# The last two output writes of a retention and soft-MoE kernel, each cut into two transfers by rows

## The chip, the cores and the metric

The kernel runs on one core of one Trainium2 chip. The metric is the device time of one execution in microseconds; lower is better.

## The reference

Two layers follow each other. The first is a linear attention with a decay per head (4 batches, 8 heads, 768 positions, 64 wide); the second is a soft mixture of experts over all 3072 tokens, with 8 experts of 4 slots each.

```python
state = gamma * state + k_t v_t^T          # per batch, head and position t
y_t   = scale * q_t @ state
x      = y as (3072 tokens, 512)
logits = x @ phi                           # 32 slots
d = softmax of logits over the tokens;  slot_input = d.T @ x
h = max(slot_input[e] @ w1[e], 0);      slot_out[e] = h @ w2[e]     # 8 experts
c = softmax of logits over the slots;   out = c @ slot_out          # (3072, 512)
```

## The kernel before, in words

The order of every engine's work is the order of the code (a manual schedule over all engines). All data moves by transfers that SyncE (SP) issues from one queue; the ones that concern us are writes of 128 partitions from SBUF to the output in HBM.

The first part of the kernel steps through the 24 pieces of the attention (4 batches by 6 chunks of 128 positions) in pairs and gathers the slots' inputs on the way; the weights `w1` and `w2` stream in beside this. Then come the experts: `hidden` (line 586) is the first layer, and the second layer is cut into three blocks of output columns, `BLOCKS` (line 36), of 256, 128 and 128. A block's second layer is 64 matmul groups into one bank (line 669). When a block is summed, the generator `finish` (line 630) takes it: it copies the sum, spreads it with one matmul (line 638), and then combines it with the weights `cT`: for each 128 output columns (`m`) and each half of the tokens (`h`) four matmuls of 384 columns (line 650), four copies out of PSUM by VectorE and ScalarE in turn (line 655) into one SBUF tile `ot` of 128 x 1536, and one write of that tile (line 656). The output in HBM is laid out with the 512 columns as rows and the 3072 tokens along a row, so each write moves 128 rows of 6144 bytes. There are 8 such writes: 4 of the first block, 2 of the second, 2 of the third. The writes of a block are spread among the matmuls of the next block; those of the third block have nothing after them.

The program ends (line 733, the end of the kernel's context) when SP has seen every transfer land and the engines have met.

Of the kernel before, what the change touches and what calls it, by code (L numbers as in the profile page):

```python
# [17 lines left out]
C = 128  # L18
# [17 lines left out]
BLOCKS = [(0, 256), (256, 128), (384, 128)]  # L36
# [8 lines left out]
PACE = (1, 1, 1, 2, 1, 2, 1, 2, 2, 0, 2, 2)  # L45
TURNED = (0, 1, 2, 3, 4, 8, 12, 14)
SIW = 48
LEAN = [i for i in range(1, NSTEP) if i in TURNED or i >= NSTEP - B]
FULL = [i for i in range(1, NSTEP) if i not in LEAN]

# [31 lines left out]
def retention_soft_moe_kernel(  # L82
# [9 lines left out]
    nc = tc.nc  # L92
# [11 lines left out]
    def large(pool):  # L104
        return pool.tile([128, 2048], F32, name="b", tag="b")

    def slot():
        return ring.tile([128, 1024], F32, name="r", tag="r")

    def small(name, shape, bufs=1):  # L110
        return cpool.tile(shape, F32, name=name, bufs=bufs)

    def bank(name, shape=(128, 512)):
        return ps.tile(list(shape), F32, name=name)
# [73 lines left out]
    def load_in(i):  # L188
# [5 lines left out]
        if i == 0:  # L194
            nc.sync.dma_start(t[:, 0:1024], first_[0])
            nc.sync.dma_start(first, first_[1])
            st[i]["v"] = first[:, K_ALL:K_ALL + 512].rearrange("p (h e) -> p h e", e=D)
        elif i in LEAN:
            nc.sync.dma_start(t[:, 0:1536], in3[LEAN.index(i)])
        else:  # L200
# [329 lines left out]
    weight_pool[0] = big  # L530
    siT = qtab.rearrange("p g t -> p (g t)")[:, 0:2 * (NK * SIW + 16)]
    nc.gpsimd.memset(siT, 0.0)
    siT = siT.rearrange("p (g x) -> p g x", g=2)
    sis = siT[:, :, 0:NK * SIW].rearrange("p g (k s) -> p g k s", s=SIW)[:, :, :, 0:16]
    si0 = qtab.rearrange("p g t -> p (g t)")
# [50 lines left out]
    def hidden(hf, g, k):  # L586
        for j in range(4):
            a = g * NK * SIW + k * SIW + 4 * j
            nc.tensor.matmul(hp[hf][32 * j:32 * j + 32, :], si0[:, a:a + NSLOT],  # L589
# [40 lines left out]
    def finish(cb, op):  # L630
        c0, w = BLOCKS[cb]
        os_ = small("os", [128, 256])
        s4 = slot()
        nc.vector.tensor_copy(os_[:, :w], op[:, :w])
        for _ in range(Y1[cb] - 1):
            yield
        rp = bank("Y0")
        nc.tensor.matmul(rp[:, :w], rep, os_[:, :w], start=True, stop=True)  # L638
        nc.vector.tensor_copy(s4[:, :w], rp[:, :w])
        for _ in range(Y2[cb] - 1):  # L640
            yield
        for m in range(w // 128):
            for h in range(2):
                ot = large(big)[:, 0:12 * C].rearrange("p (c j t) -> p c j t", j=B, t=C)
                cps = []
                for j in range(B):
                    tags = co_tags if cb < len(BLOCKS) - 1 else last_tags
                    cp = bank(tags[n_co[0] % len(tags)]).rearrange("p (c t) -> p c t", t=C)[:, 0:3]
                    n_co[0] += 1
                    nc.tensor.matmul(cp, s4[32 * j:32 * j + 32, m * 128:(m + 1) * 128],  # L650
                                     cT[32 * j:32 * j + 32, 3 * h:3 * h + 3, :], start=True, stop=True,
                                     skip_group_check=True, tile_position=(32 * j, 0))
                    cps.append(cp)
                for j in range(B):
                    (nc.scalar.copy if j % 2 else nc.vector.tensor_copy)(ot[:, :, j, :], cps[j])
                nc.sync.dma_start(out[c0 + m * 128:c0 + (m + 1) * 128, h * 12 * C:(h + 1) * 12 * C],
                                  ot.rearrange("p c j t -> p (c j t)"))
                for _ in range(BURST[cb]):
                    yield

    for cb, (c0, w) in enumerate(BLOCKS):
        if cb == len(BLOCKS) - 1:
            n_co[0] = 0
        op = bank(("A0", "A1")[cb % 2])
        units = ([(g, 4 * hf + f) for hf in range(2) for g in range(2) for f in range(4)] if cb == 0 else
                 [(g, fc) for g in range(2) for fc in range(NFC)])
        for n, (g, fc) in enumerate(units):
            for j in range(4):
                nc.tensor.matmul(op[32 * j:32 * j + 32, :w], hT[fc // 4][:, fc % 4, 4 * g + j, :],  # L669
                                 w2t[4 * g + j, cb, fc], start=(n == 0), stop=(n == len(units) - 1),  # L670
                                 skip_group_check=True, tile_position=(0, 32 * j))
            if cb == 0 and n == 2:
                hidden_t(1)
            for f in pend:
                next(f, None)
        done = finish(cb, op)
        next(done)
        for f in pend:
            for _ in f:
                pass  # L680
        pend = [done]
# [4 lines left out]
def lay_out(q, k, v, moe_phi, moe_w1, moe_w2):  # L686
# [6 lines left out]
    def nat(x):  # L693
        x = np.asarray(x).reshape(B, H, NC, C, D)
        return x.transpose(2, 0, 3, 1, 4).reshape(NSTEP, C, 512)
# [7 lines left out]
    for cb, (c0, w) in enumerate(BLOCKS):  # L703
# [3 lines left out]
        else:  # L707
# [3 lines left out]
    x = np.concatenate([kt, qt, vn, nat(k)], axis=2)  # L711
    return dict(x3=x[LEAN][:, :, 0:1536], x4=x[FULL],
                w1=w1, w2=np.concatenate(w2),
# [24 lines left out]
```

## Time and profile before

| what | before |
|---|---|
| median of 3 runs | 158.36 us (158.28 to 158.56) |
| the profiled execution's own time | 158.41 us |
| its span, first to last instruction | 156.6 us |
| TensorE busy | 144.6 us (92%) |
| DMA engines, mean share of 16 from 5 to 148 us | 0.99 to 1.02 |
| last instruction of VectorE that computes ends | 149.13 us |
| last output write issued, landed | 149.19 us, 155.5 us |

The span is what the views of the trace show; the execution's own time is 1.8 us longer. A share of the 16 DMA engines of 1.0 means that all sixteen move data; 0.5 is eight of them, 0.19 three.

### The profile page before, as it was taken

The page shows a single profiled execution, that of the slowest core. Times are in us where ns is not written, and L with a number is a line of the kernel's source. Part 1 is how long each engine was busy: PE and PEld are TensorE (multiplying, and loading weights), DVE is VectorE, ACT ScalarE, POOL GpSimd, SP SyncE. Part 2 cuts the span into 40 slices and gives each one's busy share as a digit, 9 for nine tenths or more (in the row PEclk, how much of TensorE's full clock was granted, in tenths as well). Part 3 has the DMA queues.
Part 4 walks back from the last instruction along what each step waited for, and adds up shares of the span by engine and source line. Part 5 has one row for each costly group of instructions (what it writes and reads, how often), then busy time and mean ns, then how long its engine had stood idle before and what let it go on. Part 6 is the DMA issues. An engine that isn't in the chain of part 4 may idle for free.

```text
span 156.6 us, 5484 instructions
## 1 busy us (share of the span) xinstructions
PE 144.6 (92%) x2412; PEld 107.4 (69%) x2412; DVE 77.8 (50%) x187; ACT 42.2 (27%) x100; POOL 58.8 (38%) x66
## 2 busy tenths in 40 slices
PE   7999999999999999999999979999999999999500
PEld 2688989897988789979996857864232555557200
DVE  0379337682865483768574847566010104535500
ACT  3215422333232316220613042344100001424300
POOL 1351986784936294654938283010000000000000
PEclk9999999999999999999999999999999999999985
DMA  4999999999999999999999999999999999999891
GB/s 159 421 424 421 416 419 416 416 414 419 406 423 408 423 419 410 427 398 431 404 419 412 415 411 416 400 408 421 411 428 416 423 416 416 414 415 417 348 402 78
DMA packets 9816, 62.48 MB, mean 399 GB/s; under 512 B 1088, under 2 KB 1088, under 8 KB 4544
## 3 DMA queue, kind: packets, MB, share of 16 engines
q1 hardware_dynamic: 9792, 62.13, 96.6%
q8 instruction: 19, 0.31, 0.8%
q14 instruction: 5, 0.04, 0.1%
HBM read 55.84 MB, written 6.29 MB: 397 GB/s over the span
## 4 chain that ended last, share of the span: by engine, by line
PE 92%; DVE 2%; issue 1%; DVEq 0%
PE A L227 16%; PE Y L260 15%; PE A L669 9%; PE A L304 7%; PE Y L251 6%; PE S L288 6%; PE Y L589 4%; PE A L589 4%; PE sm L328 4%; PE sm L424 3%; PE S L384 3%; PE A L206 2%; PE sm L650 2%; PE S L650 1%; PE Y L650 1%; PE Y L638 1%
## 5 line engine op out<-in xcount | busy, mean ns | idle before, releaser
L235 DVE TENSOR_TENSOR r<-A,mi 128x512 f32<-128x512 f32 (+1 forms) x50 | 30.1, 662 | 22.1 <-PE A L227 22.1
L212 POOL TENSOR_TENSOR b<-b,qtab 128x512 f32<-128x512 f32 x20 | 25.7, 1287 | 23.5 <-DMA b<-in_x_dram 18.3
L227 PE MATMUL A<-b 64*128 64x128 f32 x384 | 25.4, 280 | 0.0
L227 PEld LDWEIGHTS A<-b 64*128 64x128 f32 x384 | 22.7, 188 | 3.1 <-issue 2.0
L217 POOL TENSOR_TENSOR b<-b,kt 128x512 f32<-128x512 f32 x23 | 23.6, 1046 | 2.4 <-DMA b<-in_x_dram 2.4
L260 PE MATMUL Y<-r,b 128*64 128x128 f32 x352 | 22.5, 276 | 0.5 <-issue 0.5
L260 PEld LDWEIGHTS Y<-r,b 128*64 128x64 f32 x352 | 19.2, 137 | 2.9 <-issue 2.6
L669 PE MATMUL A<-b,r 128*32 128x128 f32 (+1 forms) x336 | 15.9, 300 | 0.0
L311 ACT COPY r<-A 128x512 f32<-128x512 f32 x23 | 12.4, 592 | 8.6 <-PE A L304 8.6
L669 PEld LDWEIGHTS A<-b,r 128*32 128x32 f32 x336 | 10.3, 109 | 6.4 <-issue 4.4
L304 PE MATMUL A<-mi,r 128*128 128x128 f32 x96 | 13.3, 278 | 0.3 <-ACT r L279 0.3
L288 PE MATMUL S<-b 128*64 128x64 f32 x304 | 11.1, 222 | 0.6 <-issue 0.6
L304 PEld LDWEIGHTS A<-mi,r 128*128 128x128 f32 x96 | 10.4, 141 | 1.7 <-ACT r L279 0.5
L288 PEld LDWEIGHTS S<-b 128*64 128x64 f32 x304 | 10.4, 138 | 0.5 <-issue 0.5
L251 PE MATMUL Y<-b,sst 64*64 64x128 f32 x304 | 10.6, 276 | 0.0
L416 POOL TENSOR_TENSOR cn<-cn,cz 128x128 f32<-128x128 f32 x6 | 2.4, 401 | 19.6 <-DVE cz L415 7.2
L280 DVE COPY r<-Y 128x512 f32<-128x512 f32 x9 | 6.2, 690 | 5.9 <-PE Y L260 5.1
L251 PEld LDWEIGHTS Y<-b,sst 64*64 64x64 f32 x304 | 8.2, 132 | 1.2
L328 PEld LDWEIGHTS sm<-r,kt 128*32 128x32 f32 x192 | 6.2, 110 | 3.3 <-issue 3.3
L408 ACT ACTIVATE cn<-cn 128x128 f32<-128x128 f32 x6 | 1.9, 310 | 21.2 <-DVE cn L407 21.2
L328 PE MATMUL sm<-r,kt 128*32 128x128 f32 x192 | 7.4, 273 | 0.0
L297 DVE TENSOR_TENSOR sst<-sst,S 128x256 f32<-128x256 f32 x16 | 6.0, 418 | 2.7 <-PE S L288 2.5
(140 smaller groups left out, 182.9 us busy)
## 6 DMA issues: line engine op xcount, KB each, us to landing
b<-in_w_dram SPq DMA_DIRECT2D x29, 1024.0 KB, 15.1
b<-in_x_dram SPq DMA_DIRECT2D x12, 1024.0 KB, 12.5
b<-in_x_dram SPq DMA_DIRECT2D x11, 768.0 KB, 10.7
out_dram<-b SPq DMA_DIRECT2D x8, 768.0 KB, 8.7
r<-in_w_dram SPq DMA_DIRECT2D x5, 512.0 KB, 11.0
b<-in_first_dram SPq DMA_DIRECT2D x1, 512.0 KB, 3.5
r<-in_first_dram SPq DMA_DIRECT2D x1, 512.0 KB, 4.3
sst<-in_w_dram SPq DMA_DIRECT2D x1, 512.0 KB, 11.7
```

The costliest lines, as they stand in the source:

```text
L212: nc.gpsimd.tensor_tensor(q, q, qtab, ALU.mult)
L217: nc.gpsimd.tensor_tensor(v, v, vsc[:, i // B, a:b].unsqueeze(2).broadcast_to([128, b - a, D]), ALU.mult)
L227: nc.tensor.matmul(s["sc"][r][:, g, :], s["kT"][half(r), g, :], s["qT"][half(r), g, :], start=True, stop=True, skip_group_check=True)
L235: nc.vector.tensor_tensor(s["A"][:, r, g:g + n], s["sc"][r][:, g:g + n], mask.unsqueeze(1).broadcast_to([128, n, C]), ALU.mult)
L251: nc.tensor.matmul(p["y"][k][b][half(half_of(r, g)), gl, :], sst[(2 * P + k) % B][half(r), g, :], s["qT"][half(r), g, :], start=(gl == 0 a ...
L260: nc.tensor.matmul(pr[P]["y"][k][g // 2][half(half_of(r, g)), g % 2, :], s["v"][:, 2 * g + r, :], s["A"][:, r, g, :], start=(P < B // 2 an ...
L288: nc.tensor.matmul(S_[half(r), k, g, :], s["kn"][:, 2 * g + r, :], s["v"][:, 2 * g + r, :], start=True, stop=True, skip_group_check=True)
L304: nc.tensor.transpose(X[k][:, g * 128:(g + 1) * 128], pr[P]["yT"][:, k, g, :], ident)
L311: (nc.scalar.copy if engines[k] == "scalar" else nc.vector.tensor_copy)(xn, pr[P]["X"][k])
L328: nc.tensor.matmul(q["ltp"][32 * j:32 * j + 32, :], phis[:, p, :], st[GRP * g + j]["yT"][:, p, :], start=(p == 0), stop=(p == NPAIR - 1), ...
L589: nc.tensor.matmul(hp[hf][32 * j:32 * j + 32, :], si0[:, a:a + NSLOT], w1t[hf, g, k][:, j * 512:(j + 1) * 512], start=(g == 0 and k == 0), ...
L669: nc.tensor.matmul(op[32 * j:32 * j + 32, :w], hT[fc // 4][:, fc % 4, 4 * g + j, :], w2t[4 * g + j, cb, fc], start=(n == 0), stop=(n == le ...
```

## The change

The third block's two writes are cut by rows into two transfers each. For the half `h` = 0 (the write ahead of the last) the cut is at row 104: transfers of 104 and 24 rows. For `h` = 1 (the last) it is at row 120: transfers of 120 and 8 rows. What is written, and from which tile, is the same; the other six writes are as before.

```diff
+LAST_ROWS = (104, 120)
...
-                nc.sync.dma_start(out[c0 + m * 128:c0 + (m + 1) * 128, h * 12 * C:(h + 1) * 12 * C],
-                                  ot.rearrange("p c j t -> p (c j t)"))
+                cuts = (0, 128) if cb < len(BLOCKS) - 1 else (0, LAST_ROWS[h], 128)
+                for a, b in zip(cuts, cuts[1:]):
+                    nc.sync.dma_start(out[c0 + m * 128 + a:c0 + m * 128 + b, h * 12 * C:(h + 1) * 12 * C],
+                                      ot[a:b].rearrange("p c j t -> p (c j t)"))
```

On SP's queue the end of the program stood as follows before: four writes of the first block, two of the second and two of the third. The name in front of the arrow is the output, `b_...` is the tile `ot`, and the brackets name what SP waits for ahead of the issue; DMAHW0 to DMAHW7 are eight landing semaphores, taken in turn.

```order
L656 DMA out_0_dram<-b_1908 128x1536 [waits DMAHW4_49,DVE_49,Activation_49]
L656 DMA out_0_dram<-b_1934 128x1536 [waits DMAHW5_49,DVE_49,Activation_49]
L656 DMA out_0_dram<-b_1960 128x1536 [waits DMAHW6_49,DVE_49,Activation_49]
L656 DMA out_0_dram<-b_1986 128x1536 [waits DMAHW7_49,DVE_49,Activation_49]
L656 DMA out_0_dram<-b_2035 128x1536 [waits DMAHW0_49,DVE_49,Activation_49]
L656 DMA out_0_dram<-b_2061 128x1536 [waits DMAHW1_49,DVE_49,Activation_49]
L656 DMA out_0_dram<-b_2113 128x1536 [waits DMAHW2_49,DVE_49,Activation_49]
L656 DMA out_0_dram<-b_2127 128x1536 [waits DMAHW3_49,DVE_49,Activation_49]
```

The same place on SP's queue with the change; the line numbers are those of the changed file.

```order
L659 DMA out_0_dram<-b_1908 128x1536 [waits DMAHW4_49,DVE_49,Activation_49]
L659 DMA out_0_dram<-b_1934 128x1536 [waits DMAHW5_49,DVE_49,Activation_49]
L659 DMA out_0_dram<-b_1960 128x1536 [waits DMAHW6_49,DVE_49,Activation_49]
L659 DMA out_0_dram<-b_1986 128x1536 [waits DMAHW7_49,DVE_49,Activation_49]
L659 DMA out_0_dram<-b_2035 128x1536 [waits DMAHW0_49,DVE_49,Activation_49]
L659 DMA out_0_dram<-b_2061 128x1536 [waits DMAHW1_49,DVE_49,Activation_49]
L659 DMA out_0_dram<-b_2113 104x1536 [waits DMAHW2_49,DVE_49,Activation_49]
L659 DMA out_0_dram<-b_2113 24x1536 [waits DMAHW3_49]
L659 DMA out_0_dram<-b_2128 120x1536 [waits DMAHW4_49,DVE_49,Activation_49]
L659 DMA out_0_dram<-b_2128 8x1536 [waits DMAHW5_49]
```

The last two rows of before have become four. The second part of each waits for no copy of its own, only for a landing semaphore's earlier use; the 120-row part has moved from the semaphore DMAHW3 to DMAHW4. No other engine's instructions change.

## Rows read from the trace of the kernel before

**Rows 1.** The page's first and second part: busy time of the engines, and the span in 40 slices of 3.9 us, with the mean busy share of the 16 DMA engines in tenths and the rate that they moved.
```profile
PE 144.6 (92%) x2412; PEld 107.4 (69%) x2412; DVE 77.8 (50%) x187; ACT 42.2 (27%) x100; POOL 58.8 (38%) x66
...
DMA  4999999999999999999999999999999999999891
GB/s 159 421 424 421 416 419 416 416 414 419 406 423 408 423 419 410 427 398 431 404 419 412 415 411 416 400 408 421 411 428 416 423 416 416 414 415 417 348 402 78
```

**Rows 2.** The end of the program in stretches (from:to in us): length, busy time of PE, PEld, DVE, ACT, POOL, granted TensorE clock, mean share of the 16 DMA engines, GB/s.
```profile
144.00:146.00 2.00, 1.43 (x38) 0.97 (x29) 0.41 (x2) 0.00 (x0) 0.00 (x0) 1.00 1.01 421
146.00:147.00 1.00, 0.77 (x12) 0.54 (x15) 0.18 (x1) 0.00 (x0) 0.00 (x0) 1.00 0.99 412
147.00:148.00 1.00, 0.80 (x12) 0.19 (x4) 0.82 (x2) 0.78 (x3) 0.00 (x0) 1.00 0.70 281
148.00:149.00 1.00, 0.00 (x0) 0.00 (x0) 1.00 (x3) 0.84 (x3) 0.00 (x0) 1.00 0.55 221
149.00:150.00 1.00, 0.00 (x0) 0.00 (x0) 0.13 (x1) 0.00 (x0) 0.00 (x0) 1.00 0.96 399
150.00:151.00 1.00, 0.00 (x0) 0.00 (x0) 0.00 (x0) 0.00 (x0) 0.00 (x0) 1.00 1.02 418
```

**Rows 3.** The same columns in short stretches of the last microseconds.
```profile
152.20:152.80 0.60, 0.00 (x0) 0.00 (x0) 0.00 (x0) 0.00 (x0) 0.00 (x0) 0.50 0.98 399
152.80:153.03 0.23, 0.00 (x0) 0.00 (x0) 0.00 (x0) 0.00 (x0) 0.00 (x0) 0.50 0.59 241
153.10:153.33 0.23, 0.00 (x0) 0.00 (x0) 0.00 (x0) 0.00 (x0) 0.00 (x0) 0.50 0.51 214
153.33:153.56 0.23, 0.00 (x0) 0.00 (x0) 0.00 (x0) 0.00 (x0) 0.00 (x0) 0.50 0.20 80
153.60:153.83 0.23, 0.00 (x0) 0.00 (x0) 0.00 (x0) 0.00 (x0) 0.00 (x0) 0.50 0.19 80
154.40:154.63 0.23, 0.00 (x0) 0.00 (x0) 0.00 (x0) 0.00 (x0) 0.00 (x0) 0.50 0.19 80
154.70:154.93 0.23, 0.00 (x0) 0.00 (x0) 0.00 (x0) 0.00 (x0) 0.00 (x0) 0.50 0.13 53
154.93:155.20 0.27, 0.00 (x0) 0.00 (x0) 0.00 (x0) 0.00 (x0) 0.00 (x0) 0.50 0.06 23
155.20:156.60 1.40, 0.00 (x0) 0.00 (x0) 0.00 (x0) 0.00 (x0) 0.00 (x0) 0.50 0.00 0
```

**Rows 4.** The last two writes: the timeline of SP (start, length, line and operation), and the view of line 656 from 147 us on (its two issues' durations, and the times from issue to landing).
```profile
148.26 1.26 SPq L656 DMA_DIRECT2D out_dram<-b  x2
L656 SPq DMA_DIRECT2D out_dram<-b x2: 332/332/333, 148.3 to 149.2; - x2
DMA to landing us min/median/max: 5.4/5.9/6.3
```

**Rows 5.** The timeline of VectorE and ScalarE, the last copies of line 655 (start and length).
```profile
147.65 1.48 DVE L655 COPY b<-A 128x384 f32<-128x384 f32 x3
148.33 0.51 ACT L655 COPY b<-Y 128x384 f32<-128x384 f32 x1
```

**Rows 6.** The waits of SP's queue from 140 us on, and the semaphore instructions of the program's end (line 733) on SP, with the first and last start.
```profile
SPq L733 <- DMA out_dram<-b: 6.0, 1, 6.0
L733 SPq EVENT_SEMAPHORE  x7: 17/28/28, 155.5 to 156.5; - x7
```

**Rows 7.** The page's third part: packets of all transfers by size, and by queue the packets, megabytes and share of 16 engines over the span.
```profile
DMA packets 9816, 62.48 MB, mean 399 GB/s; under 512 B 1088, under 2 KB 1088, under 8 KB 4544
## 3 DMA queue, kind: packets, MB, share of 16 engines
q1 hardware_dynamic: 9792, 62.13, 96.6%
q8 instruction: 19, 0.31, 0.8%
q14 instruction: 5, 0.04, 0.1%
```

## The prediction

> **What bounds the kernel now.** I read the page's slices first, then the end of the program in ever shorter stretches. The reader should see in [rows 1] that the DMA engines are full from the second slice nearly to the end, and the last slice is almost empty; TensorE is busy for 92% of the span, but the stretch that this change touches comes after its last matmul. In [rows 2] compute stops at about 149.1 us and DMA goes on alone. The last two writes are issued at 148.26 and 149.19 us and land 5.4 and 6.3 us later, at 153.7 and 155.5 [rows 4]. SP waits 6.0 us for that landing and needs 1.1 us more to end the program [rows 6]. So whatever the last landing moves, the time moves, as long as nothing else gets later than it.
>
> The short stretches [rows 3] show how the drain ends. The share of the 16 engines is 0.98 until 152.8, then 0.51 (8 engines), from 153.33 on 0.20 and 0.19 (3 engines), and this until past 154.7. So eight engines are done at about 153.0, five at about 153.5, and three at about 155.1. More than a quarter of the time from 149.1 to 155.1 is spent with three engines of sixteen. Thirteen engines have nothing to do for the last 1.5 us or more: this is the time that can be won.
>
> Why three are late: of the 16 engines' time 0.8% goes to 19 instruction blocks [rows 7], 0.008 x 16 x 156.6 / 19 = 1.06 us each on one engine. The late three stand 2.1 us behind the first eight, which is two such blocks. While the queue is full the engines never meet, so such a delay stays; only when the early ones run dry, as in 147 to 149 us with shares of 0.70 and 0.55 [rows 2], do they wait for the next write. [...]
>
> **What a row costs.** Three engines move 80 GB/s together [rows 3], so 6144 bytes take 6144 / 26.7 GB/s = 0.23 us on one engine. All 68 transfers of before have 128 rows and end in 1088 small packets, 16 each; 9792 - 1088 = 8704 = 68 x 128 are data [rows 7]. A write is thus sixteen shares of 8 rows, 1.84 us each.
>
> **What the change does to the shares.** No row shows a transfer of other than 128 rows. I assume that it is cut into equal shares of whole rows, on as many engines up to 16 as divide it, counted from the lowest: 104 = 13 x 8, 24 = 12 x 2, 120 = 15 x 8, 8 = 8 x 1. [...] Against the 16 rows per engine of the two writes of before:
> - engines 0 to 7: 8 + 2 + 8 + 1 = 19 rows, +3, +0.69 us
> - engines 8 to 11: 18 rows, +2, +0.46 us
> - engine 12: 16 rows, no change
> - engines 13 and 14: 8 rows, -1.84 us
> - engine 15: none, -3.68 us
>
> The bounds of this term are the split that changes nothing (all sixteen share, 0 us) and the one above.
>
> **The sum.** If the three late engines are 13 to 15, they finish at 155.1 - 1.84 = 153.3 or sooner. The five end at 153.5 + 0.46 = 154.0 at most if they are 8 to 12, the eight at 153.0 + 0.69 = 153.7. The last engine is then done at 154.0 in place of 155.1: -1.1 us. If one of the five is among those with three more rows it is 154.2, -0.9 us; if the five took nothing at all, 153.5 would be the floor, -1.6 us.
>
> Two more issues of 0.33 us stand on SP [rows 4]. The 24 rows are issued right behind the 104, from 148.6 to 148.95 us, before the last tile's copies end at 149.13 [rows 5], so the 120 rows go out at 149.19 as before. If that cover were gone it would cost up to 0.33 us of issue, but not of landing, since all engines are full at 150 to 151 [rows 2]. The 8 rows go out near 149.55, more than 3 us before an engine reaches them. The new waits are for landing semaphores of earlier writes; DMAHW4 and DMAHW5 were last used by the first two output writes, which a queue this full has finished well before 148 us. Those cost 0. Behind the last of them stands only the end of the program.
>
> Against the profiled execution's 158.41 us the sum is 158.41 - 1.1 = 157.3; its median of three is 0.05 lower, which leaves 157.3 us after rounding. About 0.2% (0.3 us) is what a measurement of this kernel can tell from no change.
>
> **The rivals.**
> *A late engine is one that gets more.* No row names the engine of a packet. The counts are 8, 5 and 3; with 19 blocks this is what eight engines served in turn would give (three have three, five have two, eight have none), so the late three are neighbours in some ring, but nothing says where it starts. One late engine among 8 to 11 is enough: 155.1 + 0.46, 158.9 us; among 0 to 7, +0.69, 159.1 us. That is slower. [...]
> *The cut moves no work between engines*, because each part is spread over all sixteen, or the last of the late three is engine 12 with its 16 rows kept: 158.4 us, no change. [...] For this to be the whole story the shares in [rows 3] would have to fall together, and they fall in three steps.
> *A row costs more in an uneven split*, say because two engines read from the same part of SBUF at once. Engines 8 to 11 have 18 rows and 1.1 us to lose: from 0.06 us a row (0.29 in place of 0.23) the gain is gone, and at half speed it would be 18 x 0.23 - 1.1 = 3 us worse, 161 us. For it speaks only that such splits are new here; 6 KB and 8 KB rows alike run at 410 to 420 GB/s in [rows 1].
>
> **How the numbers follow.** The late three are the three that lose rows: 0.56, 157.3 us, by itself 157.0 to 157.6. [...] A late engine gets more: 0.24, 158.9 to 159.1. No work moves, or the late one keeps its rows: 0.14, 158.2 to 158.6. A row costs more: 0.06, up to 161. Faster 0.56, within 0.2% 0.14, slower 0.30. The range that holds eight in ten must take in the slower case: 157.0 to 159.0 us.
>
> **What would show it.** Small packets: 66 x 16 + 13 + 12 + 15 + 8 = 1104 if the shares are as assumed; 1120 if all sixteen share each part. Right: no stretch with a share of 0.19 for a microsecond, a share that falls from near 0.75 straight to 0 around 154, the last landing near 154.4, and still 1.1 us from there to the end. Wrong in the first way: three engines still alone, until about 155.6. Wrong by dearer rows: a rate below 400 GB/s between 149.5 and 152 us with the share still 1.

## The result, and the profile after

The changed kernel is slower: 160.46 us median (159.28 to 161.29) against 158.46 (158.28 to 158.8), a ratio of 1.0117 with a 95% interval of 1.008 to 1.0154. The forecast was 157.3 us with a range up to 159.0. In these four runs each the changed kernel also scatters more: 2.0 us from the fastest to the slowest run, where the kernel before has 0.5. Medians here and below are of all runs; the ratios leave out one of 779.39 us (the cut at 112, below) and one of 208.47 us (the kernel before), which lie far from all others.

The page of the changed kernel, the slices of the span and the packets by size:

```profile
span 158.8 us, 5486 instructions
...
DMA  5999999999999999999999999999999999999882
GB/s 155 414 426 419 421 413 421 415 413 419 407 425 409 425 413 415 417 413 418 412 414 416 418 386 404 366 403 418 418 429 404 425 419 423 403 423 415 306 271 110
DMA packets 9832, 62.48 MB, mean 393 GB/s; under 512 B 1104, under 2 KB 1104, under 8 KB 4560
```

The 1104 small packets are those that I said would show the assumed shares: 13 + 12 + 15 + 8 beside 66 x 16. The two kernels below that cut one write each have 1097 and 1095, which is 13 + 12 and 15 + 8 by themselves beside 67 x 16. So the numbers of engines are the assumed ones. No view names an engine: that every part begins at the same, lowest engine stays an assumption, and "0 to 7", "12 to 15" and "the lowest eight" are names under it. The slices show the trouble: the last but two and the last but one have engines nearly as busy (8 and 8 tenths, against 8 and 9 in [rows 1]) but move 306 and 271 GB/s, where before they moved 348 and 402.

The end of the changed kernel in stretches of 1 us, with the columns of [rows 2]:

```profile
150.00:151.00 1.00, 0.00 (x0) 0.00 (x0) 0.10 (x1) 0.00 (x0) 0.00 (x0) 1.00 0.87 252
151.00:152.00 1.00, 0.00 (x0) 0.00 (x0) 0.00 (x0) 0.00 (x0) 0.00 (x0) 0.52 0.74 190
152.00:153.00 1.00, 0.00 (x0) 0.00 (x0) 0.00 (x0) 0.00 (x0) 0.00 (x0) 0.50 0.99 326
153.00:154.00 1.00, 0.00 (x0) 0.00 (x0) 0.00 (x0) 0.00 (x0) 0.00 (x0) 0.50 1.00 277
154.00:155.00 1.00, 0.00 (x0) 0.00 (x0) 0.00 (x0) 0.00 (x0) 0.00 (x0) 0.50 0.83 301
155.00:156.00 1.00, 0.00 (x0) 0.00 (x0) 0.00 (x0) 0.00 (x0) 0.00 (x0) 0.50 0.73 295
156.00:157.00 1.00, 0.00 (x0) 0.00 (x0) 0.00 (x0) 0.00 (x0) 0.00 (x0) 0.50 0.22 86
157.00:158.00 1.00, 0.00 (x0) 0.00 (x0) 0.00 (x0) 0.00 (x0) 0.00 (x0) 0.50 0.03 12
```

Share and rate together give what a row costs: share x 16 engines x 6144 bytes / rate. Before, at 150 to 151 us [rows 2], the rate was 418 GB/s at a share of 1.02, which is 0.24 us a row. Here it is 0.33 us over 151 to 153 and 0.38 at its dearest, and this while the engines count as busy; from 155 us on it is 0.24 to 0.25 again. Over the whole tail, from 149.2 to 157.9 us, the engines moved

```profile
q1 hardware_dynamic: 371, 1.91, 67.2%
```

which is 0.672 x 16 x 8.7 us for 311 rows (the other 60 packets are small), 0.30 us a row on average. The trace's list of single DMA packets shows what the average is made of. Of the 283 rows that start from 150 to 158 us, 196 took at most 0.24 us, as in a whole write, and 54 took from 0.4 us to 1.33 us, most of these around twice as long. Before, from 148 us on, one row of 335 took over 0.3 us. The drain no longer falls in three steps to three engines; it ends in a long slope past 157 us.

SP's own view of the four issues (durations in ns, shortest, median, longest):

```profile
L659 SPq DMA_DIRECT2D out_dram<-b x4: 313/856/2542, 149.2 to 151.5; - x4
```

Before, each took 332 to 333 ns [rows 4].

### The profile page after: what moved, and what is told of

Same layout as the page of the kernel before. It is cut to its first block, busy times and chain, and to the rows that moved or that the text cites. A ratio compares the mean times of both kernels' runs of the same rounds, so it can differ in the third digit from the quotient of the medians.

```text
span 158.8 us, 5486 instructions
## 1 busy us (share of the span) xinstructions
PE 144.6 (91%) x2412; PEld 107.3 (68%) x2412; DVE 79.4 (50%) x187; ACT 42.1 (26%) x100; POOL 58.6 (37%) x66
## 2 busy tenths in 40 slices
DMA packets 9832, 62.48 MB, mean 393 GB/s; under 512 B 1104, under 2 KB 1104, under 8 KB 4560
## 4 chain that ended last, share of the span: by engine, by line
PE 88%; DVE 4%; issue 2%; ACT 1%; DVEq 0%; ACTq 0%
PE A L228 15%; PE Y L261 13%; PE A L672 9%; PE A L305 7%; PE Y L252 6%; PE S L289 6%; PE Y L590 4%; PE A L590 4%; PE sm L329 4%; PE sm L425 3%; PE S L385 3%; PE A L207 2%; DVE r L236 2%; PE sm L651 1%; PE S L651 1%
```

## The experiments

The theories at the outset were: dear rows (a row of a cut write costs more than 0.23 us), wrong engines (the late three don't lose rows but get some), and, since the first profile also had its first output write 0.97 us later than before, a third question: whether that part is the change's at all.

**The changed kernel again, and the kernel before again.** No edit in either.

> The changed kernel once more, nothing altered. Its first profile had two pieces of extra time: the first output write was issued 0.97 us later than before (134.36 against 133.38 us), ahead of anything that the change touches, and from the issue of the last but one write to the last landing it took 8.6 in place of 7.2 us. Theory 1 (the tail is the change's, the 0.97 us is the execution's own): the first output write goes out anywhere from 133.3 to 134.4, and the tail is again 8 to 9.5 us. Theory 2 (both are the change's): 134.3 to 134.4 again. Time 159.3 to 161.3 us either way.

> The kernel before once more, for one profile: does the first output write go out later than 133.4 us with no change at all? If that moves by itself, it is anywhere up to 134.7 us; if 133.4 us is the kernel's own, it is 133.3 to 133.5 us again. The tail, from the issue of the last but one write to the last landing, is 6.5 to 7.3 us.

The changed kernel took 159.93 us against 158.56 (ratio 1.008, interval 1.0048 to 1.0112). The second profile of the kernel before had 158.6 us, and its timeline on SP (start, length, the eight output writes) is

```profile
134.52 16.14 SPq L656 DMA_DIRECT2D out_dram<-b  x8
```

against 134.35 us for the first of the changed kernel's:

```profile
134.35 19.72 SPq L659 DMA_DIRECT2D out_dram<-b  x10
```

So the first write goes out 0.2 us later in an unchanged kernel than in the changed one: this moves by itself, and the part of theory 2 that gives it to the change falls. (The changed kernel's second profile had 134.50 us, just outside what either theory named, and a tail of over 8 us again; the unchanged kernel decides it.) And it hardly matters: that profile's span is 156.8 us, 0.2 longer than the first one's. The end of the same execution shows why:

```profile
150.40:154.00 3.60, 0.00 (x0) 0.00 (x0) 0.00 (x0) 0.00 (x0) 0.00 (x0) 0.91 1.01 416
154.00:155.00 1.00, 0.00 (x0) 0.00 (x0) 0.00 (x0) 0.00 (x0) 0.00 (x0) 0.50 0.20 80
```

Three engines are alone from 154 to 155 us as in [rows 3]. The writes went out 1.1 us later and the span grew by 0.2 us: that fits three engines that had not run out of work, where a later issue takes away idle time of the other thirteen alone. (The tail that I had asked for, from the issue of the last but one write to the last landing, was 6.3 us, a little under the 6.5 to 7.3 expected.)

The traces' lists of packets allow a finer measure. From the end of the last whole write of the second block on the slowest engine to the last end packet of all, both profiles of the kernel before took 3.70 us (151.47 to 155.17 and 151.65 to 155.35), and the two of the changed kernel 5.47 and 5.51 us (152.04 to 157.50 and to 157.55). So about 1.8 us of the loss is in the tail. The other 0.4 to 0.6 us by which these two profiles are late stood ahead of the first cut row; what made it stays open.

**One cut at a time.**

```diff
-LAST_ROWS = (104, 120)
+LAST_ROWS = (104, 128)      # e2: a row count of 128 leaves the write whole
+LAST_ROWS = (128, 120)      # e3
```

> Only the write ahead of the last is cut (104 and 24 rows), the last is whole. Dear rows (rows of a cut transfer cost far more than 0.23 us, because several engines read the same part of SBUF): the rate falls well under 400 GB/s for 2 us or more behind 150 us with the engines' share near 1, and about half of the change's extra tail stays, 159.0 to 159.8 us. Only wrong engines (the late three are among those that get the 24 rows): +0.46 us, 158.9 us, with the rate at 400 GB/s or more. As I forecast (the late three lose 8 rows): 157.3 us.

> Only the last write is cut (120 and 8 rows). Dear rows: the rate falls during the 120 rows, and the long issues of 1.3 and 2.5 us on SP come back if they belong to this; 159 to 160 us. Only wrong engines: the eight lowest get one row more, 0 to +0.23 us, 158.4 to 158.6 us. As I forecast, two of the late three keep their rows: 158.4 us.

With 104 and 24 alone: 159.99 against 158.56 us, ratio 1.0077 (1.0054 to 1.0099). With 120 and 8 alone: 158.82, ratio 1.0015 (0.9996 to 1.0033). The first cut carries nearly all of the loss. Its end in one stretch of 4 us:

```profile
150.00:154.00 4.00, 0.00 (x0) 0.00 (x0) 0.00 (x0) 0.00 (x0) 0.00 (x0) 0.76 0.95 284
```

0.95 x 16 x 6144 / 284 = 0.33 us a row: dear rows, as that theory expected. I had only taken the time a little low (159.0 to 159.8). The tail as measured above is 5.43 us here, as long as with both cuts. In the kernel with the last write alone cut, the rows are as dear, but only once the whole write is through:

```profile
150.00:152.00 2.00, 0.00 (x0) 0.00 (x0) 0.00 (x0) 0.00 (x0) 0.00 (x0) 1.00 1.03 393
152.00:154.00 2.00, 0.00 (x0) 0.00 (x0) 0.00 (x0) 0.00 (x0) 0.00 (x0) 0.61 0.91 264
```

0.26 us a row, then 0.34. Eight dear rows cost 8 x 0.10 = 0.8 us, and thirteen engines had 1.6 to 2.1 us to spare before the late three [rows 3], so on those it costs nothing. What it cost in all, 0.2 us, is no more than the runs can tell from nothing, and about the one row (0.23 us) that a late engine among the lowest eight gets here. So "dear rows give 159 to 160 us" was wrong for this one: not the price, but the slack that covers it. The long issues of 1.3 and 2.5 us did not come back; the longest was 0.81 us.

**The same number of transfers, cut by columns.**

```diff
+ends = (0, 12 * C) if cb < len(BLOCKS) - 1 else (0, 6 * C, 12 * C)
+for a, b in zip(ends, ends[1:]):
+    nc.sync.dma_start(out[c0 + m * 128:c0 + (m + 1) * 128, h * 12 * C + a:h * 12 * C + b], flat[:, a:b])
```

> Both writes are cut in two by columns in place of rows: each half is 128 rows of 3072 bytes, on all sixteen engines with 8 rows each. Four transfers as in the change, but no engine gets more or less and the rows lie as in a whole write. If a second transfer as such costs time (issues, waits, landing): +0.3 us or more, 158.8 us and up. If it is the split by rows that costs: no difference, 158.3 to 158.6 us, the rate at 400 GB/s while all engines work, and three engines alone at the end as before.

158.41 against 158.56 us, ratio 0.999 (0.997 to 1.001): no change. The rate stays:

```profile
151.00:154.00 3.00, 0.00 (x0) 0.00 (x0) 0.00 (x0) 0.00 (x0) 0.00 (x0) 0.80 1.01 401
```

and SP's issues grow here too, to 0.93 us:

```profile
L659 SPq DMA_DIRECT2D out_dram<-b x4: 332/422/930, 149.6 to 151.0; - x4
```

A second transfer as such, with its issue, wait and landing, costs nothing here; the cut by rows does.

**Equal shares, cut by rows.**

```diff
-LAST_ROWS = (104, 120)
+LAST_ROWS = (64, 64)        # e6
+LAST_ROWS = (112, 112)      # e7
-cuts = ... (0, LAST_ROWS[h], 128)
+cuts = ... (0, 32, 64, 96, 128)   # e11
```

> Both writes cut by rows in the middle, 64 and 64: every part is 4 rows on each of sixteen engines, no engine gets more or less than before. [...] Rows are dear only where the shares are uneven: 158.4 to 158.8 us as with the cut by columns.

> Both writes cut at row 112: parts of 112 and 16 rows, 7 and 1 on each of sixteen engines, again no engine with more or less. If sharing a part of SBUF makes rows dear: seven rows an engine still begin at partitions that meet in part, a smaller loss, 158.8 to 160 us. If only uneven shares do: 158.4 to 158.8 us. A rate of 400 GB/s or more with 150 us passed would speak for the second.

> Both writes cut by rows into four transfers of 32 rows, 2 rows on each of sixteen engines; shares as in the whole write. If a part is slow in proportion to the neighbouring partitions that it spans, 32 is twice as slow as 64: rows of 0.8 us or more, a rate of 100 to 130 GB/s, 163 us or more. If 32 neighbouring partitions reach as much of SBUF as 64 do, the rate is 200 to 260 GB/s as with 64, and the time within 1 us of that run's, 159.5 to 161 us, with what eight issues add.

In these three every engine has as many rows as before; their small packets (1121, 1120 and 1184) are, but for one, those of sixteen engines for each part. Halves: 159.85 against 158.55 us, ratio 1.0065 (1.0043 to 1.0087). 112 and 16: 158.86, ratio 1.0006 (0.999 to 1.0022). Quarters: 159.63 against 158.63, ratio 1.0074 (1.0049 to 1.01). Their ends from 150 to 154 us, halves first:

```profile
150.00:154.00 4.00, 0.00 (x0) 0.00 (x0) 0.04 (x1) 0.00 (x0) 0.00 (x0) 0.61 0.93 255
```

then 112 and 16:

```profile
150.00:154.00 4.00, 0.00 (x0) 0.00 (x0) 0.00 (x0) 0.00 (x0) 0.00 (x0) 0.71 1.01 361
```

and quarters:

```profile
150.00:154.00 4.00, 0.00 (x0) 0.00 (x0) 0.00 (x0) 0.00 (x0) 0.00 (x0) 0.72 1.03 297
```

That is 0.36, 0.28 and 0.34 us a row. So dear rows don't need uneven shares: halves alone lose 1.0 us by the ratio (1.3 by the medians) with nothing moved, and their tail as measured above is 5.54 us, as long as the change's. And quarters are not dearer than halves, so it isn't the number of neighbouring partitions in proportion. The cut at 112 fits neither theory cleanly: its 361 GB/s is below the 400 that would speak for uneven shares, and its time is level.

Halves and quarters are much alike in their rates (255 and 297 GB/s), and 112 and 16 lose less (361). No stretch falls to half of 416 GB/s with the share near 1; single rows do: in the halves' trace, of 276 rows that start from 150 to 157.5 us, 138 took at most 0.24 us and 80 took 0.4 to 0.5, about twice as long. What makes them long is not shown: that engines read the same part of SBUF was my guess, no view shows what part an engine reads, and what the cut does on the HBM side was not tried apart. The halves' 159.85 us lie above the 158.4 to 158.8 us of rows that are dear only where the shares are uneven. The quarters' time was within what 32 partitions as good as 64 should give (159.5 to 161), their rate above it (297 against 200 to 260 GB/s).

**Which engines are late.** Small loads behind the kernel's last write tell how many of the late three are among the n lowest engines, if a transfer of n rows puts one row on each of these (the runs show the number of engines alone; that they are the lowest is assumed).

```diff
+nc.sync.dma_start(pb[0:4, 0:64], w1[0, 0, 0][0:4, 0:64])           # 256 bytes a row
+nc.sync.dma_start(pb[0:8, 64:192], w1[0, 0, 0][0:8, 64:192])       # 512 bytes
+nc.sync.dma_start(acc[0:12, 0:512], w1[0, 0, 0][0:12, 192:704])    # 2048 bytes
```

The first of these runs had loads of 8, 9, 11 and 16 rows of 512 bytes; in the last the three loads stand ahead of the 104 rows in the changed kernel, the third with 1024 bytes. The landings that I meant to read in the first run are shown for its last load only, so there too the packets are counted.

> The kernel before, and behind its last write four small loads of 512 bytes a row into an unused tile, of 8, 9, 11 and 16 rows, each on a line of its own. If a transfer of n rows uses one row on each of the n lowest engines, its landing tells when the slowest of those engines has drained its queue. The last write lands near 155.5 us. Late three are 13 to 15 (as I forecast): the loads of 8, 9 and 11 rows land 1.5 us or more ahead of the one of 16 rows. Late three are among 0 to 7: all four land together at the end. Late three are 8 to 10 or so: the 8 rows land about 2 us earlier than the other three.

> The kernel before, and behind its last write three small loads into tiles that are no longer used, of rows of 256 bytes on 4 engines, of 512 bytes on 8 and of 2048 bytes on 12 (the lowest ones). Behind about 155.2 us only the three late engines are still at work, so the packets that start there show how many of the late three are among engines 0 to 3 (packets of 256 bytes), 0 to 7 (512) and 0 to 11 (2048), beside three small end packets of the write and one for each row. By the earlier probe (9 rows and 12 small packets in the end: two late engines of 0 to 7 and one of 11 to 15, or one each of 0 to 7, 8, and 9 to 10): two packets of 512 bytes and two or three of 2048. If the late three were 13 to 15: none of any.

> The same kernel once more. If the late three are the same engines in every execution, the counts of the three sizes are those of the run before. If the turn among the eight engines goes on from execution to execution, they differ, and then no fixed split of rows could help in all of them.

> The changed kernel with the three small loads (256 bytes a row on 4 engines, 512 on 8, 1024 on 12) issued ahead of the 104 rows, behind the last whole write: which of the engines are late in this kernel? In the unchanged kernel two runs showed the same late three: none of 0 to 3, two of 4 to 7, one of 12 to 15. Same engines here: of the packets that start from about 151.7 us on, while only the late three still have the last whole write before them, four are of 512 or 1024 bytes and three small end packets belong to the write, four to the loads. The wrong-engines theory in full (all three take 8 rows of the 104 and 2 of the 24) needs all three among 0 to 11: five or six packets. Time as the changed kernel, 159.3 to 161.5 us.

The packets that started from 154.6 us on, when only the late three were at work, in the first of the two equal runs,

```profile
DMA packets 15, 0.03 MB, mean 12 GB/s; under 512 B 7, under 2 KB 9, under 8 KB 15
```

and in the second:

```profile
DMA packets 15, 0.03 MB, mean 12 GB/s; under 512 B 7, under 2 KB 9, under 8 KB 15
```

Two packets lie between 512 bytes and 2 KB: two late engines are among the lowest eight. The seven small ones are three end packets of the write and four of the loads: with two of the 512-byte load there are two left for the others, so none or one is of 4 engines. A 256-byte row would itself be an eighth small packet, so none; two are of 12 engines. So under that assumption the late three are two of engines 4 to 7 and one of 12 to 15, in both. The first run (157.6 us span, 159.41 us, its loads were issued later) showed from 155 us on

```profile
DMA packets 26, 0.04 MB, mean 18 GB/s; under 512 B 12, under 2 KB 21, under 8 KB 26
```

9 rows of 512 bytes: 4 + 4 + 1 for the same set, though this run alone would allow others. In the changed kernel, from 151.4 to 152.4 us, it is

```profile
DMA packets 55, 0.27 MB, mean 273 GB/s; under 512 B 7, under 2 KB 11, under 8 KB 55
```

four rows (in the trace's list two of 512 and two of 1024 bytes) and seven small packets, the first of the two counts expected: the same groups as before. The stretch begins 0.3 us earlier than I had set it, but from 150.6 us on the counts are the same 7 and 11. So both of my guesses about which engines are late fall, 13 to 15 and "all three among 0 to 11" alike, as far as the assumption holds. No run here tells single engines apart.

No version beat the kernel before. Three were level with it: two of them (columns; 112 and 16) move no work, and 120 and 8 moves little.

## Why the prediction was wrong, point by point

*What bounds the end* was right: SP waits for the last landing, three engines are late and the others have time to spare. The second profile of the kernel before makes it firmer, since 1.1 us later writes moved its span by 0.2 us only. Why these three are late, the 19 instruction blocks, was not tried.

*Which engine gets how many rows* was right in the number of engines, by the 1104 small packets. That the parts all begin at the same engine, from which the 19, 18, 16, 8 and 0 rows and so the -1.1 us follow, no run shows; what the runs show in its place is 13, 12, 15 and 8 end packets and a tail 1.8 us longer.

*What a row costs* is the step that failed. I took 0.23 us a row from whole writes and gave a dearer row 0.06, "for it speaks only that such splits are new here". The runs put it at 0.33 to 0.38 us in the stretches where most engines work on a write of 128 rows that is cut into 104 and 24, 120 and 8, halves or quarters, and at 0.30 over the changed kernel's whole tail. My own threshold stood in that paragraph: from 0.29 us a row the gain is gone. With this mean price the lowest eight have 19 x 0.30 - 16 x 0.23 = 2.0 us more than before, an estimate; the first eight would end at 155.0, about when the late three did before. The sign that I had named, a rate below 400 GB/s with the share still 1, came at 152 to 154 us (326 and 277), behind a share of 0.87 and 0.74. (My side remark that all rows run at 410 to 420 GB/s in [rows 1] was too narrow: the full slices have 398 to 431.)

*Who is late* failed too. Under the same assumption the packet counts make two of the late three engines that take three rows more, +0.69 us, and put one among 12 to 15, where a row count can fall or stay. I gave "a late engine gets more" 0.24 and the upper end of the list 0.56, and no row told the one from the other. By itself this would have ended at 155.1 + 0.69 = 155.8 us, 159.1 us in all, so it was enough to turn the forecast's sign; the halves, which move no rows, show that the dear rows were enough as well. On an engine that is late and among the lowest eight the two add up: 2.0 us by the estimate above, 155.1 + 2.0 = 157.1, against 1.8 us measured in the tail and 157.5 for the last packet. In both profiles of the changed kernel the two engines that finish last end with a share of a single row, which only the 8-row part has, so both are among the eight that carry it, as this asks. How the 1.8 us divides between the two causes is not shown, for the halves lose as much in the tail with no row moved.

*The issues of 0.33 us* were wrong in size (up to 2.5 us). That they cost nothing is shown up to 0.93 us only: the cut by columns had such issues and lost nothing. Whether the 2.5 us in the changed kernel delayed a start was not tested alone; at 151 to 152 us its share of 0.74 leaves about four engines without work, which may be those that the 104 rows leave out and that wait for the 120.

*The rival with the wrong sign* that came true was the third (a row costs more), at a lower price than the 3 us of half speed, and with it the worse case of the first (a late engine among 0 to 7).

## What to carry to other kernels

Here, cutting a write of all 128 partitions by rows made rows dearer even where each engine kept its share (0.36 against 0.24 us for halves), while cutting it by columns cost nothing (158.41 against 158.56 us). Before moving work off a late engine, find out which engine it is; small transfers of n rows behind the real ones, each with its own row size, show in the counts of packets which group it belongs to, if they and the real ones begin at the same engine, as was assumed here. And a stall that is covered by slack (eight dear rows, 0.2 us in all; writes that are issued 1.1 us later, 0.2 us of span) is nearly free until the slack is used up, so look at the slack of each engine before adding costs up.

## What the runs showed of the hardware that I had not expected

Rows of 6144 bytes from 32 or 64 neighbouring partitions, on sixteen engines: 0.34 and 0.36 us a row at a share near 1, against 0.24 for whole writes. An engine counts as busy for all of that time, so a DMA share of 1.0 doesn't say that the rate is full: in the changed kernel it was 277 GB/s at a share of 1.00 from 153 to 154 us, before 418 at 1.02.

Some issues on SP took 0.8 to 2.5 us in place of 0.33 when more transfers were put on a queue with work left, for cuts by rows and columns and for the small loads of e5 alike (two of its four are shown; its last took 0.33 us). The cause stays open:

```profile
L660 SPq DMA_DIRECT2D probe<-in_w_dram x1: 972/972/972, 150.7 to 150.7; - x1
L661 SPq DMA_DIRECT2D probe<-in_w_dram x1: 863/863/863, 151.8 to 151.8; - x1
```

The packet counts of four executions of three different kernels all agree with one set of late engines, two of 4 to 7 and one of 12 to 15, and three of the four ask for it, if transfers of n rows use the n lowest engines.
